# First attention block's outputs and last transposes moved into the MLP's PSUM banks, whole keys in 22 visits, a product at full height, 140 pairs of noughts, new ranks

## The chip, the cores and the metric

One Trainium2 chip, one core of it. The metric is device time in microseconds (us) of one execution. The kernel before takes 1190.74 us (median of three runs, 1190.32 to 1192.26). The profiled execution took 1190.45 us, its span from the first to the last instruction is 1188.7 us, so 1.75 us lie outside the span.

## The reference, cut to what matters

```
scores = (q @ k.T) / 8                                  # 4 batches, 8 heads, 576 rows, 64 wide
scores = where(scores >= rowmax(scores) - tau, scores, -1e9)
attn = exp(scores - rowmax(scores));  attn /= sum(attn) + 1e-9
x = (attn @ v), heads side by side                      # 2304 rows x 512
h = x @ w1_in;   g = max(h, 0) + alpha * min(h, 0);   x = g @ w1_out   # 512 -> 2048 -> 512
h = x @ w2_in;   g = h - tanh(h);                     out = g @ w2_out # 512 -> 2048 -> 512
```

Everything is computed in 32-bit floats.

## The kernel before

**Attention.** The 576 query rows of a head are cut into 256 + 256 + 64. A *visit* is one head and one block of 256 rows as two tiles of 128; 64 visits, numbered 0 to 63, eight heads to a block. Two heads' last 64 rows make one tile, a *left*; there are 16 of them. A tile goes through: scores on TensorE (`scores`, L644, lefts L730) into one of two PSUM tiles `sc` of two banks each; row maximum (L513), threshold (L516), exponential (L519, ScalarE), mask with row sum (L525), guard and reciprocal (L530, L533), scaling by the reciprocal; five transposes on TensorE, four into the bank `pt` (L569) and the last 64 keys' (L572) into the first bank of `sc`; copies out of PSUM; products with v (L663 or L671 and L672, lefts L753), written to `acc` for visits 0 to 7 and to the second bank of `sc` afterwards; then the output is put into `x`.

**Two ways to multiply.** A product in split form writes each operand as a high part (copy to the type fp32r) and a low part (the difference) and adds three fp32r products. A *raw* operand (`raw(k)`, `RAW` visits) is loaded whole and multiplied as float32 in one go; `one(k)` (`WHOLE` visits) does the same for v and the attention weights. With `raw` the copies `k_hi`, `k_lo` and the differences `q_lo`, `left_lo` fall away, with `one` `v_lo` and the low parts of the transposed weights. A float32 product shows as two TensorE records each.

**Weights of the MLPs.** Each MLP's weights come in 32 pieces of 512 KB, as raw 64-bit words (`piece`). A piece is made up by six steps; the two that only VectorE does are L347 (`ends_`) and L352 (`middle`), the differences are mostly GpSimd's (L284).

**MLP.** 18 blocks of 256 rows (9 in each MLP), eight *pairs* to a block. A pair is 24 first products into the bank `hp` (`h_pair`, L842), an activation on ScalarE and VectorE, a high and a low part, and the second products into the banks `acc` (`acc_pair`, L903 and L895). The first MLP's blocks run beside the attention of later blocks.

**Noughts.** `warm` multiplies zeros (`qc`) into `acc[1]`, two matmuls a time, 80 times (L960). They have the last rank of all and stand wherever the planner found nothing else for TensorE.

**The order.** Nothing is scheduled on the chip. `Plan.order` plays the program through with a cost for each operation, a lag between engines and a rank; at each step it issues the operation that can start first, the lowest rank among those, and so fixes the order of every engine's queue. Each queue, the loads' queue SP included, runs strictly in that order. The ranks are the numbers at the head of the file (`TA`, `PA`, `PB`, `MLP_PE`, `OFF` and so on). The planner also keeps two engines out of one PSUM bank at a time (the `banks` of an operation).

Of the kernel before, what the change touches and what calls it, by code (L numbers as in the profile page):

```python
# [37 lines left out]
TA = 17.2217  # L38
PA, PB = 8.596, 3.314
MLP_PE = 409.5389  # L40
MLP_G = -417.911
PREP = -31.4411
WHOLE = 17
RAW = 6
FLEX_R = 1
FLEX_HI = 1
POOL_PEN = 0.0393
ACT_PEN = 0
# [6 lines left out]
XR = 6.0872  # L55
FLEX = 1
T_WARM = 0.3
N_WARM = 80
DVE_PEN = 0.4374
OFF = {"S": 6.59, "M": -68.93, "TH": -138.48, "E": 14.87, "X": -28.47, "R": -62.2, "N": -8.46, "T": 123.89, "H": -217.07, "L": -80.02, "AV": 130.4, "XC": -36.36, "XH": -117.34}  # L60
# [169 lines left out]
def attention_mlp_mlp(ctx: ExitStack, tc: tile.TileContext, kv, q0, q1, tau, w1i, w1o, alpha, w2i, w2o, out):  # L230
# [30 lines left out]
    qc = tpool.tile([P, 2, P], F32R, name="qc")  # L261

# [26 lines left out]
    def either(dve, pool):  # L289
        return {"DVE": dve, "POOL": pool} if FLEX else {"POOL": pool}  # L290
# [101 lines left out]
    begun = {}  # L392

# [3 lines left out]
    def one(k):  # L397

        return whole(*visits[k])

    def raw(k):

        return k < RAW

    def prep(v, rank):
        b, qb, h = visits[v]
        k = brings[v]
        rkv, rq, ks, vs, qs = ("rkv", k), ("rq", v), ("ks", k), ("vs", k), ("qs", v)
# [26 lines left out]

        def k_hi(e):
            copy(e, take(tpool, ks, [P, 2, S], F32R, "ks", BUFS["ks"])[:, 0], T[rkv][:, :KW])
# [4 lines left out]
        def rows(x):  # L442
            return x[:, KW:].rearrange("p (c d) -> p c d", c=5)

        def v_hi(e):
            x = take(tpool, vs, [P, 5, 2, D], F32R, "vs", BUFS["vs"])[:, :, 0, :]
            copy(e, x.bitcast(F32) if one(k) else x, rows(T[rkv]))
# [25 lines left out]

        add({"SYNC": rate * QH}, rank - 6, load_q, [ROOM], [rq], takes=[("rq", rq)], lag=DMA_LAG)
        if new and raw(k):
            add({"SYNC": rate * KW}, rank - 6, load_whole_k, [ROOM], [(*ks, 0)], takes=[("ks", ks)], lag=DMA_LAG)
            add({"SYNC": rate * VW}, rank - 6, load_whole_v, [ROOM], [(*vs, 0)], takes=[("vs", vs)], lag=DMA_LAG)
        elif new:
            k_raw, v_raw = (*rkv, 0), (*rkv, 1)
            n = add({"SYNC": rate * KW}, rank - 6, load_k, [ROOM], [k_raw], takes=[("rkv", rkv)], lag=DMA_LAG)  # L480
            add({"SYNC": rate * VW}, rank - 6, load_v, [ROOM], [v_raw], lag=DMA_LAG, after=[n])
            add(any_of(0.58, 0.37, 0.64), rank, k_hi, [k_raw, ROOM], [(*ks, 0)], takes=[("ks", ks)])
            add(either(0.68, 1.42), rank, k_lo, [k_raw, (*ks, 0), ROOM], [(*ks, 1)])
# [3 lines left out]
        if qb:  # L487
            lc = ("qc", 0, h % 2)
# [3 lines left out]
        if new and not raw(k):  # L492
            add({"ACT": 0.36, "DVE": 0.4, "POOL": 0.5} if FLEX_HI else {"POOL": 0.5}, rank, v_hi, [v_raw, ROOM], [(*vs, 0)], takes=[("vs", vs)])
            if not one(k):
                add(either(0.4, 0.87), rank, v_lo, [v_raw, (*vs, 0), ROOM], [(*vs, 1)])

    HALVES = (slice(0, D), slice(D, P))
# [61 lines left out]

    def turned(tile, j, s, rank, g, g5, w, left, half):  # L560

        cols = slice(0, P) if left else slice(j * P, (j + 1) * P)
        p5 = sc[s][:D, :P]
        p5k, e0 = ("sc", s, "p5"), ("e", (tile, j))
        bank = [("sc", s, 0)]
# [12 lines left out]
        def pieces(x):  # L578
            return x.rearrange("p (c s) -> p c s", s=D)

        def hi_last(e):
            if g5 not in T:
                take(tpool, g5, [P, BLK], F32R, "eT5", BUFS["eT5"])
            x = T[g5][half] if left or w else T[g5][:D]
            if left and not w:
                copy(e, parts(x, 0), pieces(p5))
            else:
                copy(e, x[:, cols].bitcast(F32) if w else x[:, cols], p5)

        def lo_last(e):  # L590
            if left:
                sub(e, parts(T[g5][half], 1), pieces(p5), parts(T[g5][half], 0))
            else:
                sub(e, T[g5][D:P, cols], p5, T[g5][:D, cols])
# [23 lines left out]
        add({"PE": 0.06}, rank + OFF["T"], turn_last, [e0, ("const", 2), ROOM], [p5k], bank)  # L618
# [12 lines left out]
    def attend(v, rank):  # L631
# [15 lines left out]
        add({"PE": 1.05 if raw(k) else 0.8}, rank + OFF["S"], scores, [*ks_parts(k), *q_read, ROOM], [("sc", s, "s") for s in range(2)],  # L647
            [("sc", s, c) for s in range(2) for c in range(2)])
        softmax(v, 2, (0, 1), rank)
        pk, po = out_of(v)  # L650

        last = HALVES[pk[1]]
# [21 lines left out]
        add({"PE": 2.4 if w else 1.06}, rank + OFF["AV"], products, [*reads, ROOM], [pk, ("products", v)], pk_bank(pk))  # L674
# [22 lines left out]
        begun[xt] = add({"ACT": 0.38}, rank + OFF["XC"], x_copy, [pk, ROOM], [xk], pk_bank(pk),  # L697
                        takes=[("xt", xt)] if v % 2 == 0 else [], after=[begun[xt]] if v % 2 else [])
        if not w:
            add({"DVE": 0.4}, rank + OFF["XC"], x_add, [pk, ROOM], [xk], pk_bank(pk))  # L700
# [6 lines left out]
    def out_of(v):  # L707

        if v < H:
            return ("acc", v % 2), acc[v % 2][:, :BLK]  # L710
        return ("sc", v % 2, "po"), sc[v % 2][:, 768:]

    def pk_bank(pk):
        return [("acc", pk[1])] if pk[0] == "acc" else [("sc", pk[1], 1)]

    def attend_left(v, rank):
# [5 lines left out]

        def scores(e):
# [8 lines left out]
        reads = [x for k in ks_ for x in ks_parts(k)] + [("qc", 0, a) for a in range(2)] + [("const", 1)]  # L732
        add({"PE": sum(0.98 if raw(k) else 0.53 for k in ks_)}, rank + OFF["S"], scores, [*reads, ROOM], [("sc", s, "s")],
            [("sc", s, c) for c in range(2)])
# [96 lines left out]
    def h_pair(p, rank):  # L831
# [3 lines left out]
        for k in range(2):  # L835
            f = f0 + k
            for n0 in range(0, 12, 12 // GRP):
                now = todo[n0:n0 + 12 // GRP]

                def emit(e, now=now, n0=n0, k=k, f=f):  # L840
                    for n, (c, part, x) in enumerate(now):
                        e.matmul(  # L842
                            hp[:, k, :], lhsT=weight(l, "i", part, f // 4)[:, c, (f % 4) * P:(f % 4 + 1) * P],
                            rhs=T[f"x{x}", m][:, c, :], start=(n0 + n == 0), stop=(n0 + n == 11),
                        )

                reads = {("w", (l, "i", f // 4), c, part) for c, part, _ in now} | {(f"x{x}", m, c) for c, _, x in now}
                add({"PE": 0.118 * len(now)}, rank + MLP_PE, emit, sorted(reads, key=str), [("hp", 0)] + [("begun", m)] * (f == n0 == 0), [("hp", 0)])
# [35 lines left out]
    def acc_pair(p, rank):  # L884
        m, f0 = p // NPAIR, 2 * (p % NPAIR)
        l = m // NBLK
        for k in range(2):
            f = f0 + k
            for t in range(2):
# [20 lines left out]
                add({"PE": 0.705}, rank + MLP_PE, emit, [*reads, ("gh", p), ("gl", p)], [("acc", t)], [("acc", t)])  # L910
# [45 lines left out]
    add({"POOL": 0.46}, 0, clear, [], [("const", 1)] + [("qc", 0, a) for a in range(2)])  # L956
# [114 lines left out]
```

## Time and profile before

| | |
|---|---|
| median of three runs | 1190.74 us |
| profiled execution, its span | 1190.45 us, 1188.7 us |
| TensorE busy | 1152.9 us, 97% of the span |
| VectorE, ScalarE, GpSimd busy | 662.1, 650.9, 555.4 us |
| mean granted TensorE clock | 0.992 of 2.4 GHz |

The busy time of TensorE counts overlapping matmuls once, but it also counts matmuls that run at half the clock, and the noughts. What a stretch is worth must be read from the stretch: the attention of the first block comes first, with no MLP work to fill its waits; then attention and the first MLP run side by side until about 690 us; from there the MLPs are alone.

### The profile page before, as it was taken

To read this page: it belongs to the slowest core of one execution; us is meant where nothing else is said; L and a number is where in the kernel's file an instruction comes from. 1 tells how busy PE (TensorE), PEld (TensorE's weight loads), DVE (VectorE), ACT (ScalarE), POOL (GpSimd) and SP (SyncE) were. 2 spreads that over 40 slices of the span, in tenths; PEclk is the share of its full clock that TensorE was granted. 3 is DMA by queue.
4 is the path that set the end of the run, shared out by engine and by line. 5 is a ranking of instruction groups with operands and counts; after the bars stand their busy time and mean duration, and the time that the engine had idled before them with its cause. 6 is when DMAs were issued, how large, how long until landed. Compare 5 with 4: busy or idle time off the path is not lost.

```text
span 1188.7 us, 22011 instructions
## 1 busy us (share of the span) xinstructions
PE 1152.9 (97%) x8593; PEld 1045.4 (88%) x8593; DVE 662.1 (56%) x1393; ACT 650.9 (55%) x1265; POOL 555.4 (47%) x535
## 2 busy tenths in 40 slices
PE   9879998999999999999999999999999999999998
PEld 7548886999999989999999999999899899999997
DVE  6688785887878788778878666755111111111110
ACT  6677886666667767667666556665222222232221
POOL 4656664643645524556436366777232233223221
PEclk9889999999999999999999999999999999999999
DMA  7443432111113111122111144442010010010000
GB/s 219 133 151 103 135 113 77 56 58 41 59 39 90 57 48 38 54 63 73 55 41 55 36 148 151 156 154 89 2 36 22 15 36 12 25 37 1 19 18 18
DMA packets 51272, 81.13 MB, mean 68 GB/s; under 512 B 14560, under 2 KB 29920, under 8 KB 51168
## 3 DMA queue, kind: packets, MB, share of 16 engines
q1 hardware_dynamic: 51168, 79.73, 21.5%
q8 instruction: 67, 1.10, 0.4%
q14 instruction: 37, 0.30, 0.1%
HBM read 69.74 MB, written 9.96 MB: 67 GB/s over the span
## 4 chain that ended last, share of the span: by engine, by line
PE 86%; DVE 6%; ACT 4%; issue 2%; DMA 1%; POOL 0%; SPq 0%; ACTq 0%; DVEq 0%; POOLq 0%
PE hp L842 32%; PE acc L895 17%; PE acc L903 15%; PE sc L644 5%; PE pt L569 4%; PE sc L671 4%; PE sc L753 2%; ACT eT L279 2%; PE sc L663 1%; PE sc L572 1%; PE acc L663 1%; DVE e L525 1%; PE sc L730 1%; DVE st L513 1%; DVE rw L347 1%
## 5 line engine op out<-in xcount | busy, mean ns | idle before, releaser
L842 PE MATMUL hp<-x,ihi 128*128 128x256 f32 x2304 | 429.3, 285 | 1.6 <-DVE mr L863 1.6
L842 PEld LDWEIGHTS hp<-x,ihi 128*128 128x128 f32 x2304 | 358.2, 189 | 11.7 <-issue 2.8
L284 POOL TENSOR_TENSOR gl<-mr,gh 128x512 fp32r<-128x512 f32 x144 | 193.1, 1341 | 345.5 <-ACT gh L279 339.6
L842 PE MATMUL hp<-x,ilo 128*128 128x256 f32 x1152 | 323.7, 281 | 0.0
L861 DVE TENSOR_TENSOR mr<-hp,mr 128x512 f32<-128x512 f32 x72 | 49.8, 691 | 328.9 <-ACT mr L854 326.5
L842 PEld LDWEIGHTS hp<-x,ilo 128*128 128x128 f32 x1152 | 217.5, 189 | 0.0
L903 PE MATMUL acc<-gh,ohi 128*128 128x256 f32 x576 | 169.4, 294 | 0.0
L854 ACT ACTIVATE mr<-hp 128x512 f32<-128x512 f32 x72 | 43.1, 598 | 223.6 <-PE hp L842 223.6
L903 PE MATMUL acc<-gl,ohi 128*128 128x256 f32 x576 | 161.9, 281 | 0.0
L903 PE MATMUL acc<-gh,olo 128*128 128x256 f32 x576 | 161.6, 281 | 0.0
L513 DVE TENSOR_REDUCE st<-sc 128x1 f32<-128x576 f32 x144 | 106.4, 753 | 56.2 <-PE sc L644 33.4
L279 ACT ACTIVATE gh<-mr 128x512 fp32r<-128x512 f32 x133 | 84.0, 632 | 83.6 <-DVE mr L861 50.2
L525 DVE SCALAR_TENSOR_TENSOR e<-sc,st,e 128x576 f32<-128x576 f32 x144 | 115.9, 812 | 22.3 <-ACT e L519 13.6
L895 PE MATMUL acc<-ohi,gl 128*128 128x512 f32 x288 | 113.8, 395 | 0.0
L895 PE MATMUL acc<-olo,gh 128*128 128x512 f32 x288 | 113.7, 395 | 0.0
L895 PE MATMUL acc<-ohi,gh 128*128 128x512 f32 x288 | 113.5, 394 | 0.0
L519 ACT ACTIVATE e<-sc,st 128x576 f32<-128x576 f32 x144 | 104.9, 734 | 14.0 <-DVE st L513 11.3
L903 PEld LDWEIGHTS acc<-gh,ohi 128*128 128x128 f32 x576 | 108.7, 189 | 2.1 <-issue 2.0
L903 PEld LDWEIGHTS acc<-gl,ohi 128*128 128x128 f32 x576 | 108.7, 189 | 0.0
L903 PEld LDWEIGHTS acc<-gh,olo 128*128 128x128 f32 x576 | 108.5, 188 | 0.0
L279 ACT ACTIVATE eT<-pt 128x512 fp32r<-128x512 f32 (+1 forms) x144 | 85.6, 595 | 27.6 <-PE pt L569 23.0
L569 PE MATMUL pt<-ident,e 128*128 128x128 f32 x576 | 89.3, 278 | 8.1 <-ACT eT L279 3.9
(82 smaller groups left out, 1926.3 us busy)
## 6 DMA issues: line engine op xcount, KB each, us to landing
rkv<-in_kv_dram SPq DMA_DIRECT2D x50, 288.0 KB, 2.8
rw<-in_w1i_dram SPq DMA_DIRECT2D x16, 512.0 KB, 4.8
rw<-in_w1o_dram SPq DMA_DIRECT2D x16, 512.0 KB, 4.6
rw<-in_w2i_dram SPq DMA_DIRECT2D x16, 512.0 KB, 4.2
rw<-in_w2o_dram SPq DMA_DIRECT2D x16, 512.0 KB, 3.3
rkv<-in_kv_dram SPq DMA_DIRECT2D x50, 160.0 KB, 2.8
rq<-in_q_dram SPq DMA_DIRECT2D x160, 32.0 KB, 2.1
x1d<-o SPq DMA_DIRECT2D x18, 256.0 KB, 2.1
```

The lines of the kernel that those rows point to most:

```text
L279: e.activation(out=out_, in_=in_, func=AF.Copy, **({} if scale is None else {"scale": scale}))
L284: e.tensor_tensor(out=out_, in0=in_, in1=hi.bitcast(F32), op=ALU.subtract)
L513: e.tensor_reduce(out=T[st][:, 0, j:j + 1], in_=x(s), axis=AX.X, op=ALU.max, negate=True)
L519: e.activation(out=take(tpool, ("e", tile, j), [P, S], F32, "e", BUFS["e"]), in_=x(s), func=AF.Exp, bias=T[st][:, 0, j:j + 1], scale=1.0)
L525: e.scalar_tensor_tensor(out=w_, in0=x(s), scalar=T[st][:, 1, j:j + 1], in1=w_, op0=ALU.is_ge, op1=ALU.mult, accum_out=T[st][:, 2, j:j + 1])
L569: e.transpose(pt[:, c, :], T["e", tile, j][:, c * P:(c + 1) * P], ident)
L644: e.matmul(sc[j][:, 192:192 + S][:, c], lhsT=q_[p], rhs=k_[p, c], start=(n == 0), stop=(n == len(ops) - 1))
L671: e.matmul(po, lhsT=vf[:, c], rhs=T[g][part][:, c, :], start=(c + part == 0), stop=False)
L842: e.matmul(hp[:, k, :], lhsT=weight(l, "i", part, f // 4)[:, c, (f % 4) * P:(f % 4 + 1) * P], rhs=T[f"x{x}", m][:, c, :], start=(n0 + n == ...
L861: e.tensor_tensor(out=T[r], in0=hp, in1=T[r], op=ALU.subtract)
L895: e.matmul(acc[t], lhsT=g[:, k, t * P:(t + 1) * P], rhs=w, start=(f == 0 and n == 0), stop=(f == NF - 1 and n == 2),)
L903: e.matmul(acc[t][:, (c % 2) * BLK:(c % 2 + 1) * BLK], lhsT=w[:, c * P:(c + 1) * P], rhs=g[:, k, :], start=(f == 0 and n == 0 and c % 2 == ...
```

## The change

It sets `RAW` from 6 to 22 (keys and queries whole in visits 0 to 21) and `WHOLE` from 17 to 14. The lefts of the first batch take both heads' keys, loaded once more into a `rkv` buffer, 64 rows each, against a block-diagonal tile `qz` of 128 rows, in two float32 matmuls of 128 rows. In the first block both outputs lie in the bank `acc[0]`, side by side, and the last keys' transposes in `hp`, not in `sc`. In the lefts with split products, the last keys' weights lie high part over low part (128 rows) and are multiplied second, 64 columns wide, in place of 64 rows by 128 columns at the end. The noughts go from 80 pairs to 140, and all ranks and some of the planner's costs are other numbers. The diff, cut to its core:

```diff
-TA = 17.2217
-MLP_PE = 409.5389
-WHOLE = 17
-RAW = 6
+TA = 13.2318
+MLP_PE = 552.3152
+WHOLE = 14
+RAW = 22
...
-N_WARM = 80
+N_WARM = 140
...
+    qz = tpool.tile([P, P], F32, name="qz")
...
+        half = HALVES[h % 2] if raw(k) else slice(0, P)
+
         def left_hi(e):
-            x = qc[:, h % 2, col]
-            copy(e, x.bitcast(F32) if raw(k) else x, T[rq][:, P:], scale=qscale)
+            copy(e, qz[half, col] if raw(k) else qc[:, h % 2, col], T[rq][half, P:], scale=qscale[half])
...
+        def load_two(e):
+            x = take(tpool, kab, [P, KW + VW], F32, "rkv", BUFS["rkv"])
+            for a in range(2):
+                e.dma_start(out=x[HALVES[a], :KW], in_=kv[b, h + a][HALVES[a], :KW])
...
     def turned(tile, j, s, rank, g, g5, w, left, half):
 
         cols = slice(0, P) if left else slice(j * P, (j + 1) * P)
-        p5 = sc[s][:D, :P]
-        p5k, e0 = ("sc", s, "p5"), ("e", (tile, j))
-        bank = [("sc", s, 0)]
+        p5k, p5, bank = (("sc", s, "p5"), sc[s][:D, :P], [("sc", s, 0)]) if left or tile >= H else (("hp", s), hp[:D, s, :P], [("hp", 0)])
+        e0 = ("e", (tile, j))
...
         def lo_last(e):
-            if left:
-                sub(e, parts(T[g5][half], 1), pieces(p5), parts(T[g5][half], 0))
-            else:
-                sub(e, T[g5][D:P, cols], p5, T[g5][:D, cols])
+            sub(e, T[g5][D:P, cols], p5, T[g5][:D, cols])
...
     def out_of(v):
 
         if v < H:
-            return ("acc", v % 2), acc[v % 2][:, :BLK]
-        return ("sc", v % 2, "po"), sc[v % 2][:, 768:]
-
-    def pk_bank(pk):
-        return [("acc", pk[1])] if pk[0] == "acc" else [("sc", pk[1], 1)]
+            return ("acc", ("po", v % 2)), acc[0][:, v % 2 * BLK:][:, :BLK], HALVES[0], [("acc", 0)]
+        return ("sc", v % 2, "po"), sc[v % 2][:, 768:], HALVES[v % 2], [("sc", v % 2, 1)]
...
         def scores(e):
-            ops = []
-            for a, k in enumerate(ks_):
-                q_, k_ = qc[:, a], T["ks", k]
-                ops += [(q_[HALVES[s]].bitcast(F32), k_[HALVES[s], 0])] if raw(k) else [(q_, k_[:, 0]), (q_, k_[:, 1])]
+            if both:
+                ops = [(qz, T[kab])]
+            else:
+                ops = [(qc[:, a], T["ks", k][:, part]) for a, k in enumerate(ks_) for part in range(2)]
...
-                for c in range(5):
-                    e.matmul(
-                        dst, lhsT=vf[:, c] if c < 4 else vf[last, c],
-                        rhs=etf[:, c, c_] if c < 4 else et5f[last, c_], start=(c == 0), stop=(c == 4),
-                    )
+
+                for n, c in enumerate((0, 4, 1, 2, 3)):
+                    if c < 4:
+                        out_, l_, r_ = dst, vf[:, c], etf[:, c, c_]
+                    elif w:
+                        out_, l_, r_ = dst, vf[last, c], et5f[last, c_]
+                    else:
+                        out_, l_, r_ = dst[:, :D], vf[:, c], et5f[:, a * D:(a + 1) * D]
+                    e.matmul(out_, lhsT=l_, rhs=r_, start=(n == 0), stop=(n == 4))
```

The ranks move nearly every instruction. The first place is TensorE's queue in the first block. In the kernel before, from the last of the 160 noughts on, behind visit 4's scores, to visit 5's scores (L663 are products of visits 1, 2 and 3, L569 and L572 transposes, L644 scores):

```order
L960 MATMUL acc_92<-qc 128x256 x40
L663 MATMUL acc_92<-eT_303,vs 64x256 x4
L663 MATMUL acc_92<-eT_318,vs 64x256
L569 MATMUL pt<-ident,e 128x128 x4
L572 MATMUL sc_89<-ident,e 64x128
L572 MATMUL sc_90<-ident,e 64x128
L663 MATMUL acc_91<-eT_536,vs 64x256 x4
L663 MATMUL acc_91<-eT_542,vs 64x256
L569 MATMUL pt<-ident,e 128x128 x8
L663 MATMUL acc_92<-eT_584,vs 64x256 x4
L663 MATMUL acc_92<-eT_576,vs 64x256
L644 MATMUL sc_89<-ks,qs 128x320
```

And now, the same visit 4's scores (L655), visit 3's transposes (L589, L592) with noughts (L976) between them, and visit 3's products (L673):

```order
L655 MATMUL sc_90<-ks,qs 128x320
L655 MATMUL sc_91<-ks,qs 128x320
L655 MATMUL sc_90<-ks,qs 128x256
L655 MATMUL sc_91<-ks,qs 128x256
L589 MATMUL pt<-ident,e 128x128 x4
L592 MATMUL hp<-ident,e 64x128
L976 MATMUL acc_93<-qc 128x256 x2
L592 MATMUL hp<-ident,e 64x128
L976 MATMUL acc_93<-qc 128x256 x6
L589 MATMUL pt<-ident,e 128x128 x4
L976 MATMUL acc_93<-qc 128x256 x8
L673 MATMUL acc_92<-eT_531,vs 64x256 x4
```

Before, three visits' products stand between the scores of visits 4 and 5 and no nought comes after them; now each visit in the first block has this one pattern (scores, the visit before's transposes, its products), with 14 to 26 noughts among them, 230 up to the scores of visit 9, and the last of the 280 behind visit 12.

The second place is TensorE's queue at the products of the first left of the second batch. Before, with the transpose (L572) that follows:

```order
L753 MATMUL sc_90<-eT_3448,vs 128x128 x4
L753 MATMUL sc_90<-eT_3464,vs 128x128
L753 MATMUL sc_90<-eT_3448,vs 128x128 x4
L753 MATMUL sc_90<-eT_3464,vs 128x128
L572 MATMUL sc_90<-ident,e 64x128
```

And now:

```order
L771 MATMUL sc_91<-eT_3426,vs 128x128
L771 MATMUL sc_91<-eT_3437,vs 128x64
L771 MATMUL sc_91<-eT_3426,vs 128x128 x4
L771 MATMUL sc_91<-eT_3437,vs 128x64
L771 MATMUL sc_91<-eT_3426,vs 128x128 x3
L589 MATMUL pt<-ident,e 128x128 x4
```

Still ten matmuls; the two with 64 rows (the fifth and the tenth, which the order prints only by their output's shape) are now 128 rows high and 64 columns wide, and second of each five.

## Rows read from the trace of the kernel before

**Rows 1.** The page: busy time; granted clock and GB/s in 40 slices

```profile
PE 1152.9 (97%) x8593; PEld 1045.4 (88%) x8593; DVE 662.1 (56%) x1393; ACT 650.9 (55%) x1265; POOL 555.4 (47%) x535
...
PEclk9889999999999999999999999999999999999999
...
GB/s 219 133 151 103 135 113 77 56 58 41 59 39 90 57 48 38 54 63 73 55 41 55 36 148 151 156 154 89 2 36 22 15 36 12 25 37 1 19 18 18
```

**Rows 2.** Stretches: length, busy time by engine, granted clock, DMA share, GB/s

```profile
0.00:92.10 92.10, 77.19 (x433) 53.18 (x434) 64.50 (x124) 62.57 (x126) 50.32 (x56) 0.91 0.52 162
92.10:224.00 131.90, 126.57 (x986) 106.75 (x986) 100.11 (x207) 99.98 (x206) 79.68 (x80) 1.00 0.34 104
224.00:690.00 466.00, 456.42 (x3859) 432.24 (x3858) 363.74 (x898) 313.28 (x651) 225.66 (x259) 1.00 0.18 54
690.00:1188.70 498.70, 492.75 (x3321) 453.27 (x3319) 133.76 (x166) 175.07 (x286) 199.72 (x143) 1.00 0.17 55
```

**Rows 3.** Timeline of VectorE: start us, us; thresholds of tiles 0, 4, 5, 9, 24

```profile
8.86 0.23 DVE L516 TENSOR_SCALAR st<-st,atau 128x2 f32<-128x2 f32 x1
...
35.62 1.21 DVE L516 TENSOR_SCALAR st<-st,atau 128x2 f32<-128x2 f32 x1
...
58.74 0.61 DVE L516 TENSOR_SCALAR st<-st,atau 128x2 f32<-128x2 f32 x1
...
92.13 0.79 DVE L516 TENSOR_SCALAR st<-st,atau 128x2 f32<-128x2 f32 x1
...
224.14 0.38 DVE L516 TENSOR_SCALAR st<-st,atau 128x2 f32<-128x2 f32 x1
```

**Rows 4.** Chain that ended last, 0 to 100 us: start us, us, what

```profile
39.33 1.94 DMA rq<-in_q_dram
...
41.64 0.35 ACT qc L279
...
72.00 1.38 POOL ks L284
```

**Rows 5.** Timeline of TensorE in the first block: start us, us, instruction

```profile
17.89 1.24 PE L644 MATMUL sc<-ks,qs 64*128 64x320 f32 x8
...
33.13 5.04 PE L960 MATMUL acc<-qc 128*128 128x256 f32 x40
38.10 2.51 PE L663 MATMUL acc<-eT,vs 128*64 128x256 f32 x10
...
51.05 4.12 PE L663 MATMUL acc<-eT,vs 128*64 128x256 f32 x10 [0.97 <-ACT eT L279]
...
61.46 1.07 PE L644 MATMUL sc<-ks,qs 64*128 64x320 f32 x12
```

**Rows 6.** VectorE by line, 0 to 92.1 us: busy us, mean ns, idle before

```profile
L513 DVE TENSOR_REDUCE st<-sc 128x1 f32<-128x576 f32 x20 | 14.6, 750 | 11.5 <-PE sc L644 10.8 <-PE sc L572 0.7
L525 DVE SCALAR_TENSOR_TENSOR e<-sc,st,e 128x576 f32<-128x576 f32 x18 | 14.3, 814 | 6.7 <-ACT e L519 6.2
L347 DVE SCALAR_TENSOR_TENSOR rw<-rw 128x512 int32<-128x512 int32 x16 | 13.9, 867 | 2.8 <-ACT rw L342 1.5 <-POOL rw L344 1.3
L352 DVE SCALAR_TENSOR_TENSOR tw<-tw,rw 128x512 int32<-128x512 int32 x16 | 12.9, 809 | 0.7 <-DVE st L533 0.4
L516 DVE TENSOR_SCALAR st<-st,atau 128x2 f32<-128x2 f32 x9 | 3.8, 424 | 0.2
L530 DVE TENSOR_SCALAR st<-st 128x2 f32<-128x2 f32 x9 | 3.2, 359 | 0.2
```

**Rows 7.** Chain, 640 to 690 us

```profile
640.19 1.00 PE sc L644 x12
...
648.62 0.96 PE sc L671 x8
...
650.41 0.44 PE pt L569 x4
...
682.20 1.50 PE sc L753 x10
```

More of the change, by code (lines that the diff above doesn't have):

```diff
@@ L446, in v_hi @@
             x = take(tpool, vs, [P, 5, 2, D], F32R, "vs", BUFS["vs"])[:, :, 0, :]
-            copy(e, x.bitcast(F32) if one(k) else x, rows(T[rkv]))
+            copy(e, x, rows(T[rkv]))
         def v_lo(e):
@@ L487, in prep @@
         if qb:
-            lc = ("qc", 0, h % 2)
+            lc = ("qz" if raw(k) else "qc", 0, h % 2)
+            if raw(k) and h % 2 == 0:
+                add({"SYNC": rate * KW}, rank - 6, load_two, [ROOM], [(*kab, 0)], takes=[("rkv", kab)], lag=DMA_LAG)
             add({"ACT": 0.24}, rank, left_hi, [rq, ("const", 0), ROOM], [lc])
@@ L491, in prep @@
                 add({"DVE": 0.2}, rank, left_lo, [rq, ROOM], [lc])
[L492 to L497, printed above, removed]
+        if new and not one(k):
+            add(any_of(0.36, 0.4, 0.5), rank, v_hi, [v_raw, ROOM], [(*vs, 0)], takes=[("vs", vs)])
+            add(either(0.4, 0.87), rank, v_lo, [v_raw, (*vs, 0), ROOM], [(*vs, 1)])
     CHUNKS = (slice(0, 320), slice(320, S))
@@ L583, in hi_last @@
                 take(tpool, g5, [P, BLK], F32R, "eT5", BUFS["eT5"])
-            x = T[g5][half] if left or w else T[g5][:D]
-            if left and not w:
-                copy(e, parts(x, 0), pieces(p5))
-            else:
-                copy(e, x[:, cols].bitcast(F32) if w else x[:, cols], p5)
+            x = T[g5][half, cols].bitcast(F32) if w else T[g5][:D, cols]
+            copy(e, x, p5)
         def lo_last(e):
-            if left:
-                sub(e, parts(T[g5][half], 1), pieces(p5), parts(T[g5][half], 0))
-            else:
-                sub(e, T[g5][D:P, cols], p5, T[g5][:D, cols])
+            sub(e, T[g5][D:P, cols], p5, T[g5][:D, cols])
         def hi(e):
@@ L646, in attend @@
         q_read = [("qs", v, 0)] if raw(k) else [("qs", v, 0), ("qs", v, 1)]
-        add({"PE": 1.05 if raw(k) else 0.8}, rank + OFF["S"], scores, [*ks_parts(k), *q_read, ROOM], [("sc", s, "s") for s in range(2)],
+        add({"PE": 1.27 if raw(k) else 1.09}, rank + OFF["S"], scores, [*ks_parts(k), *q_read, ROOM], [("sc", s, "s") for s in range(2)],
             [("sc", s, c) for s in range(2) for c in range(2)])
         softmax(v, 2, (0, 1), rank)
-        pk, po = out_of(v)
-        last = HALVES[pk[1]]
+        pk, po, last, bank = out_of(v)
         reads = []
@@ L672, in products @@
             e.matmul(po, lhsT=vf[:, 4], rhs=T[g5], start=False, stop=True)
-        add({"PE": 2.4 if w else 1.06}, rank + OFF["AV"], products, [*reads, ROOM], [pk, ("products", v)], pk_bank(pk))
+        add({"PE": 2.4 if w else 1.06}, rank + OFF["AV"], products, [*reads, ROOM], [pk, ("products", v)], bank)
         m = 2 * b + qb
@@ L721, in attend_left @@
         g, g5 = ("eT", -v - 1), ("eT5", -v - 1)
+        both = all(raw(k) for k in ks_)
+        assert both or not any(raw(k) for k in ks_)
+        kab = ("rkv", -v - 1)
         def scores(e):
-            ops = []
-            for a, k in enumerate(ks_):
-                q_, k_ = qc[:, a], T["ks", k]
-                ops += [(q_[HALVES[s]].bitcast(F32), k_[HALVES[s], 0])] if raw(k) else [(q_, k_[:, 0]), (q_, k_[:, 1])]
+            if both:
+                ops = [(qz, T[kab])]
+            else:
+                ops = [(qc[:, a], T["ks", k][:, part]) for a, k in enumerate(ks_) for part in range(2)]
             for n, (q_, k_) in enumerate(ops):
@@ L730, in scores @@
                     e.matmul(sc[s][:, 192:192 + S][:, c], lhsT=q_, rhs=k_[:, c], start=(n == 0), stop=(n == len(ops) - 1))
-        reads = [x for k in ks_ for x in ks_parts(k)] + [("qc", 0, a) for a in range(2)] + [("const", 1)]
-        add({"PE": sum(0.98 if raw(k) else 0.53 for k in ks_)}, rank + OFF["S"], scores, [*reads, ROOM], [("sc", s, "s")],
-            [("sc", s, c) for c in range(2)])
+        reads = [(*kab, 0)] if both else [x for k in ks_ for x in ks_parts(k)]
+        reads += [("qz" if both else "qc", 0, a) for a in range(2)] + [("const", 1)]
+        add({"PE": 1.0 if both else 1.07}, rank + OFF["S"], scores, [*reads, ROOM], [("sc", s, "s")], [("sc", s, c) for c in range(2)])
         softmax(-v - 1, 1, (s,), rank)
```

61 lines of the change are left out of this document (35 added, 26 removed).

## The prediction

> **What bounds the kernel now.** I read the page first. TensorE is busy 97% of the span, the others half of it [rows 1], so time can only come from work TensorE needn't do, or from a place where its busy time is no use: noughts, and matmuls at half the clock. The clock row has such a place, the 8, 9 and 8 at the start [rows 1]. The table by stages then says how much: in the first 92.1 us TensorE is busy 77.2 us at a mean clock of 0.91; in the next 131.9 it idles 5.3 us, in the 466 after that 9.6 us, and in the last 498.7 us, the MLPs alone, 6 us, most of it the tail [rows 2]. So the later stages are TensorE's own work and the first one is not.
>
> What paces the first stage I read from VectorE's thresholds, one to a tile: tiles 0 to 4 go at (35.6 - 8.9) / 4 = 6.7 us each, the step to tile 5 takes 23.1 us, and tile 9 comes at 92.1, that is 8.4 us each for the last four [rows 3]. The reader is to see the cause of the gap in the chain: ScalarE's copy for the left queries (`qc`) stands in its queue ahead of visit 1's copies and waits for a load that lands at 41.3 us [rows 4], and behind it three visits' products go one after the other. With the noughts used up at 38.1 us (the last 40 end where the products begin) a float32 product takes 4.12 us where it took 2.51 [rows 5]; the stretch around it is where the clock row dips. No engine is full: VectorE is busy 64.5 of 92.1 us [rows 2] and waits mostly for scores and exponentials [rows 6].
>
> **The change part by part.**
>
> *The first block, up to tile 9's threshold.* The new order has one pattern per visit, no `qc` copy ahead of transposes, noughts until visit 12, no key copies or differences for visits 6 to 9 (one `ks` difference held GpSimd 1.38 us on the chain [rows 4]), and the last keys' transposes in another bank than the scores. VectorE's work to this point, counted in the new order: 20 maxima, 18 masks, 15 and 14 of the two weight steps, 10 thresholds, 9 guards. At the means per instruction (busy over count) of this stage [rows 6] that is 14.6 + 14.3 + 13.0 + 11.3 + 4.2 + 3.2 = 60.6 us, some 3 us more with reciprocals and the masks' accumulator reads, which have no row here; I take 63. It starts about 7 us in (the first threshold at 8.9 follows two maxima of 0.73 us), so tile 9 can't be before 70 us. From the other side, nothing may be won: 92. I take the pace that the trace shows where the noughts lasted, 6.7 us a visit with 1.25 pairs of weight steps each (5 in 4 visits by the order). Now there are 15 in 9 visits, 1.65. The 0.4 more, at 0.87 + 0.81 us, make 0.7 us, so 7.4 us a visit: 8.9 + 0.4 (the alphas' load now stands ahead of the first queries) + 9 x 7.4 = 76. Gain 16 us, between 0 and 22.
>
> Its cover: TensorE's own content up to there must stay under this. Eight float32 products at 2.51, ten raw scores at 1.24 [rows 5], eight visits' eight transposes at 0.11 [rows 7] are 20 + 12 + 7 = 39 us; 230 noughts at 4.97 / 40 = 0.124 us [rows 5] are 28.5. That is 68 us of the 76, so noughts are hidden in the waits only if these are where the planner thinks. If the pace were bounded elsewhere they cost nothing; if a wait is shorter than its noughts, up to 1 us a visit.
>
> *From tile 9 to tile 24 (132.0 us before [rows 3]).* The same attention work and the same MLP pairs by the order (516 first-size matmuls up to there in both). 50 noughts more, 6.2 us. They can fill the 5.3 us that TensorE idles there [rows 2]; between none and all, I take half, -2.6. Three visits' products leave float32: 2.51 becomes nine at 0.12 [rows 5, 7], -1.4 each, -4.3. Twelve more visits' scores, 10 to 21, become raw: in one view 1.24 against 1.07 [rows 5], +2.0. Their fall of VectorE and GpSimd work is off the path, as is the new low part of the three visits' weights: VectorE is busy 100 of 132 us [rows 2], some 7 us more fit. One left gets split products, -0.7 at most. Sum +0.6, between -5 and +5. The first batch's lefts take two 128-row float32 products; no row has that form, the nearest is 1.24 us for a raw visit's scores [rows 5]. I take no change, and 1 us either way for the four.
>
> *The lefts' products.* Twelve lefts. Ten matmuls take 1.50 us on the chain, while four transposes of the same 128 columns take 0.44, and nine products of 256 columns go at 0.12 each [rows 7]. At 0.11, ten would be 1.10. So the two with 64 rows cost 0.40 us a left beyond their length, and full height should return it: 12 x 0.40 = 4.8. Below: nothing, if the excess is a wait for the last copy. Above: with the two matmuls at half length, 0.11 more, 6.1 us.
>
> The Trainium skill (TensorEngine Tiling, Key Properties) says that a change of tiling mode drains TensorE. By that rule the 0.40 us is the drain at each of the two 64-row matmuls, and the whole of it goes; without it the excess could stay as a wait, and the term would be 0. The same skill (TensorE: Matmul & The Clock Gate, section LDWEIGHTS (loading the stationary operand)) gives loading the stationary operand a time that goes with its columns alone, 107 ns for 128, an estimate at its 1.2 columns per ns; the 0.11 us of the 128-column transposes [rows 7] agrees. By that rule the 64-column matmul is no shorter than the others, which speaks against the upper end, 6.1.
>
> *The rest.* From tile 24 the order is in step with the one before (within 24 first-size matmuls of MLP work at every third tile). Some 90 high parts of the MLP move from ScalarE to GpSimd; beside MLP work alone GpSimd is busy 200 of 499 us [rows 2], so two pairs ahead cover it. Nothing, between -3 and +3. If that cover is gone, the next late thing is a second product waiting on its low part.
>
> Sum against the profiled execution: 1190.45 - 16 + 0.6 - 4.8 = 1170. Its own time is 0.3 us under the median of the runs, which is nothing here.
>
> **The rivals.**
>
> *Loads set the pace (slower).* Up to tile 9 the new order must bring about 17 pieces of 512 KB, eight visits' keys, values and queries of 512 KB and the rest, some 13.8 MB; that takes 63 us at the 219 GB/s of the first slice, but 97 us at the 133 to 151 of the next two [rows 1]. Then tile 9 comes at 97, 5 us later than before, and the noughts behind it fill nothing: 1190.45 + 5 + 3.2 - 4.8 = 1194. It turns slower than before once tile 9 passes 94. For it: one queue issues every load and the raw keys go straight into it. Against it: the DMA share is 0.52 over that stage [rows 2], so those slices waited for buffers rather than for bandwidth.
>
> *The first block gains little.* The order's regularity is the planner's, and the chip's waits put the same 30-odd us back. Tile 9 at 88 to 92: 1182 to 1186. For it: at 6.7 us a visit VectorE was no fuller than later. Against it: the 23.1 us step is one misplaced wait and two slow products [rows 3 to 5], and both their causes are gone.
>
> *VectorE never waits.* Tile 9 at 70, and the better spaced order takes the idle 5.3 us too: 1190.45 - 22 - 3 - 6 = 1159.
>
> *No drain.* The lefts give nothing: 1175; inside the forecast's range.
>
> **How the numbers follow.** The forecast, 1164 to 1178 about 1170, 0.60; little gain, 1178 to 1188, 0.16; VectorE full, below 1164, 0.12; loads, slower, 0.12. About 2.4 us, 0.2%, is what a measurement here can tell from no change. Faster by more: 0.60 + 0.12 and nearly all of the 0.16, less a little, 0.84; within: 0.05; slower: 0.11. The range leaves out the slower case and the far end of the fast one: 1158 to 1189.
>
> **What would show it.** Right: tile 9's threshold at 71 to 82 us, tiles 0 to 9 in even steps of 7 to 8 us, no 8 in the clock row after the first slice, float32 products at 2.5 us throughout; tile 24 at 203 to 213; ten left products at 1.1 us on the chain; the last 500 us as they were. Wrong: thresholds that follow loads, TensorE waiting for SP's loads in the first 90 us; noughts on the chain beyond a few us, which would say they are longer than the waits; a left's products still at 1.5; a gain that is there at tile 24 and gone at tile 79.

## The result, and the profile after

The changed kernel takes 1180.68 us (median of 4 runs, 1180.2 to 1181.29) against 1191.13: ratio 0.9912, 95% interval 0.9895 to 0.9929, 10.4 us faster where 20.7 were forecast (1170 against the 1190.7 known then), and 2.7 us above the range of 1164 to 1178. The profiled execution took 1180.95 us, its span 1179.2.

The page of the changed kernel, the rows that answer to [rows 1]:

```profile
PE 1150.1 (98%) x8620; PEld 1049.2 (89%) x8620; DVE 678.1 (58%) x1388; ACT 575.0 (49%) x1132; POOL 602.9 (51%) x640
...
PEclk9999999999999999999999999999999999999999
...
GB/s 192 181 151 165 150 103 73 58 24 60 39 59 90 58 25 55 43 91 55 42 41 55 41 186 134 127 162 90 1 36 37 1 37 27 11 36 7 13 19 18
```

The dip in the clock row is gone. ScalarE does 76 us less work, GpSimd 48 us more, VectorE 16 us more.

Timeline of VectorE, thresholds of tiles 0, 4, 5, 9 and 24 of the changed kernel, against [rows 3]:

```profile
10.18 0.23 DVE L536 TENSOR_SCALAR st<-st,atau 128x2 f32<-128x2 f32 x1
...
41.55 0.23 DVE L536 TENSOR_SCALAR st<-st,atau 128x2 f32<-128x2 f32 x1
47.84 0.63 DVE L536 TENSOR_SCALAR st<-st,atau 128x2 f32<-128x2 f32 x1
...
78.47 0.70 DVE L536 TENSOR_SCALAR st<-st,atau 128x2 f32<-128x2 f32 x1
...
212.21 0.23 DVE L536 TENSOR_SCALAR st<-st,atau 128x2 f32<-128x2 f32 x1
```

The 23.1 us step is gone, tile 9 comes at 78.5 instead of 92.1. The chain of waits in the first block, against [rows 4]:

```profile
5.23 6.41 DMA rw<-in_w1i_dram
...
15.93 1.81 DVE tw L353
...
20.78 2.44 PE acc L673 x10
23.22 1.17 PE sc L655 x8
24.39 0.67 PE acc L976 x4
```

No copy for left queries is on it and no GpSimd difference of keys; a float32 product takes 2.44 us each time on this chain, which is the 2.51 of the timeline in [rows 5]. What is new here is a wait for the first weight piece, 6.41 us, ahead of visit 1. Further on the chain has a left's products, 1.50 us in [rows 7], as

```profile
653.62 1.26 PE sc L771 x10
```

A threshold stands in VectorE's queue, and at tile 24 it comes 2.6 us after the tile's first score matmul before, 6.7 us after it now. So I account for the time at TensorE's own marks: the first score matmul of tiles 9 and 24, the last product of the last left, the end. The MLP matmuls issued up to tile 24's mark are 516 in both. Stretches between these marks, first of the kernel before (us, busy time of TensorE, its weight loads, VectorE, ScalarE, GpSimd, granted clock, DMA share, GB/s):

```profile
0.00:88.60 88.60, 74.42 (x410) 51.10 (x410) 61.33 (x117) 59.61 (x119) 47.91 (x53) 0.90 0.54 168
88.60:221.50 132.90, 126.85 (x984) 106.52 (x983) 101.05 (x211) 101.32 (x208) 80.00 (x80) 1.00 0.33 101
221.50:683.40 461.90, 452.32 (x3829) 428.03 (x3828) 364.49 (x898) 311.34 (x645) 225.05 (x256) 1.00 0.18 54
683.40:1188.70 505.30, 499.35 (x3374) 459.80 (x3373) 135.25 (x170) 178.63 (x293) 202.42 (x147) 1.00 0.17 55
```

and of the changed kernel:

```profile
0.00:75.20 75.20, 72.08 (x470) 55.57 (x470) 57.26 (x111) 52.51 (x107) 39.02 (x51) 1.00 0.63 188
75.20:205.50 130.30, 127.36 (x961) 108.34 (x960) 105.12 (x211) 94.35 (x194) 78.04 (x83) 1.00 0.40 121
205.50:672.70 467.20, 450.05 (x3814) 424.82 (x3814) 378.93 (x899) 294.11 (x609) 241.11 (x289) 1.00 0.18 52
672.70:1179.20 506.50, 500.59 (x3381) 460.49 (x3380) 136.84 (x170) 134.04 (x222) 244.74 (x218) 1.00 0.17 55
```

| stretch | before, us | after, us | difference | forecast |
|---|---|---|---|---|
| to tile 9's scores | 88.6 | 75.2 | -13.4 | -16 |
| to tile 24's scores | 132.9 | 130.3 | -2.6 | +0.6 |
| to the last left's products | 461.9 | 467.2 | +5.3 | -4.8 |
| to the end | 505.3 | 506.5 | +1.2 | 0 |

Up to tile 24 the gain is 16.0 us, against a forecast of 15.4. The shortfall is all behind it: the third stretch was to get 4.8 us shorter and got 5.3 longer, with TensorE idle for 467.2 - 450.05 = 17.2 us instead of 9.6. In VectorE's column about as many instructions (898 and 899) take 14 us more.

### The profile page after: what moved, and what is told of

It is laid out like the page before. It is cut to its first block, busy times and chain, and to the rows that moved or that the text cites. A ratio compares the mean times of both kernels' runs of the same rounds, so it can differ in the third digit from the quotient of the medians.

```text
span 1179.2 us, 22125 instructions
## 1 busy us (share of the span) xinstructions
PE 1150.1 (98%) x8620; PEld 1049.2 (89%) x8620; DVE 678.1 (58%) x1388; ACT 575.0 (49%) x1132; POOL 602.9 (51%) x640
## 4 chain that ended last, share of the span: by engine, by line
PE 78%; DVE 11%; ACT 4%; issue 3%; POOL 2%; DMA 1%; SPq 0%; ACTq 0%; DVEq 0%; POOLq 0%
PE hp L857 30%; PE acc L910 17%; PE acc L918 13%; PE sc L655 4%; PE pt L589 4%; PE sc L681 3%; DVE e L545 3%; DVE eT L285 2%; DVE st L533 1%; PE sc L592 1%; PE sc L771 1%; DVE st L550 1%; PE acc L673 1%; PE acc L976 1%; DMA rw<-in_w1i_dram 1%
## 5 line engine op out<-in xcount | busy, mean ns | idle before, releaser
L282 POOL TENSOR_SCALAR gh<-mr 128x512 fp32r<-128x512 f32 x100 | 63.3, 633 | 299.4 <-DVE mr L876 215.9
L533 DVE TENSOR_REDUCE st<-sc 128x1 f32<-128x576 f32 x144 | 106.3, 753 | 38.6 <-PE sc L655 23.1
L280 ACT ACTIVATE e<-e,st 128x576 f32<-128x576 f32 x97 | 72.9, 770 | 61.1 <-DVE st L553 60.1
L280 ACT ACTIVATE eT<-pt 128x512 fp32r<-128x512 f32 (+1 forms) x144 | 85.4, 593 | 30.6 <-PE pt L589 26.4
```

The costliest lines, as they stand in the source:

```text
L280: e.activation(out=out_, in_=in_, func=AF.Copy, **({} if scale is None else {"scale": scale}))
L282: e.tensor_scalar(out=out_, in0=in_, scalar1=1.0, scalar2=1.0, op0=ALU.mult, op1=ALU.mult)
L533: e.tensor_reduce(out=T[st][:, 0, j:j + 1], in_=x(s), axis=AX.X, op=ALU.max, negate=True)
```

## The experiments

In each, "before" is the kernel before on the same chip (1190.1 to 1191.1 us); ratios are to it, with their 95% intervals. "The stage" is the third stretch of the table, taken at the same marks, in one trace of each kernel. The tile marks given below are VectorE's thresholds, other than where TensorE's are named. Since the kernel before ranges over 1 us from set to set, smaller differences between runs of different sets aren't told apart.

### The lefts' products in either order

In the kernel before, only the lefts' last keys as in the changed kernel:

```diff
-    for c in range(5): e.matmul(dst, lhsT=vf[:, c] if c < 4 else vf[last, c], ...)
+    for n, c in enumerate((0, 4, 1, 2, 3)): ...  # c == 4: dst[:, :D], lhsT=vf[:, 4], rhs=et5f[:, a * D:(a + 1) * D]
```

> The kernel before, its order untouched, with only the lefts' last keys changed: copied at full height and multiplied with 128 rows. If TensorE's time in the stage of tiles 24 to 79 is the time of that stage (theory A, the prediction's), 12 lefts give back 0.40 us each: about 1186.3 against 1191.1, ten left products at 1.1 us on the chain, and idle time of TensorE as before (8.9 us between tiles 24 and 79). If the saved time turns into waits whatever the order (theory B), 1191 within 1 us, with the products at 1.1 us and 4 to 5 us more idle. If the saving isn't there at all (theory C), the products stay at 1.5 us.

1187.7 us, ratio 0.998 (0.9971 to 0.999). The stage takes 458.1 us instead of 461.9.

The reverse, the changed kernel with the old lefts' products:

> The changed kernel, its order untouched, with the old lefts' products (last keys at half height). Theory A: 4.5 to 4.8 us slower than the changed kernel, 1185.3. Theory B, that this order's waits take the saving: 0 to 1 us slower, 1181 to 1182, with 4 to 5 us less idle of TensorE between tiles 24 and 79 than the 15.1 us of the changed kernel.

1183.0 us, 0.9935 (0.9923 to 0.9947), 2.4 us over the changed kernel. The stage takes 469.1 us instead of 467.2. So the saving is real in both orders (theory C falls), in the stage's traces 3.8 us in the old and 1.9 in the new: TensorE's busy time falls by 5.6 and 3.4 us, and 1.8 and 1.5 of that becomes idle time. By the medians it is 2.4 us in either, so whether the orders differ in it is open. The excess stood at the matmuls of 64 rows: in the stage's lefts TensorE's next matmul starts 0.12 us after a 128-row one, but the 64-row one starts 0.205 us after the one ahead of it, and the one behind it 0.254 us after it. And with either kind of lefts the new order is slower in this stage: 469.1 against 461.9, 467.2 against 458.1, that is 7.2 to 9.1 us for nearly the same matmuls (visits 20 and 21 take eight records for their scores in place of twelve, and six second products of the MLP lie behind the last mark instead of ahead of it).

### Noughts

```diff
     def warm(e):
+        warmed.append(0)
+        if len(warmed) > 80: return
```

> The changed kernel with the 60 last pairs of noughts issuing nothing, all else in its order. If the noughts after the first 80 pairs stand on the path (theory D), those up to tile 9 go (some 70 matmuls of 0.12 us, of which the chain shows about half): tile 9 comes 3 to 6 us earlier than 78.5 and the time is 1175 to 1178. If they hold the clock (theory E, the prediction's), the clock row shows an 8 or less in the third slice, float32 products of the visits after the 80th pair take up to 4.1 us instead of 2.4, and tile 9 comes 2 to 8 us later, 1183 to 1189. Hidden in waits and not needed for the clock: 1181 within 1 us.

1179.4 us, 0.9904 (0.9891 to 0.9917); tile 9 at 77.4, tile 24's scores 2.9 us earlier than in the changed kernel, clock row all 9. In this run the last 60 pairs cost 1 to 3 us (the ratios' intervals overlap) and the clock didn't need them. Another run without them, in the section on late transposes, has an 8 in the second slice, so that is not shown to hold every time. Without any:

> The changed kernel without any noughts. If only the first 80 pairs hold the clock (theory E in its weaker form, after the run without the last 60): an 8 or less in the first three slices of the clock row, float32 products of the first visits at 4 to 5 us instead of 2.4, tile 9 at 84 to 95, the time 1186 to 1196. If the clock needs none of them: tile 9 at 70 to 76 and the time 1172 to 1178.

1183.7 us, 0.9945 (0.9926 to 0.9964); tile 9 at 81.2, tile 24 at 212.8. The page:

```profile
PE   4778999999999999999999999999999999999998
...
PEclk9899999999999999999999999999999999999999
```

One slice at 8; two of the first block's eight products take 4.07 and 4.64 us in the timeline, the others 2.51. That is a loss of 2.7 us at tile 9 that is down to 0.6 at tile 24. The six runs lie between 1180.4 and 1188.9, where the changed kernel's four lie within 1.1 us: the noughts buy an even clock more than time.

### The first weight pieces

The two first pieces' loads behind visit 1's, and their steps behind a mark in tile 0 or tile 1:

```diff
+    for group, mark in ((early_loads, behind["v", 1]), (early_steps, behind["mask", 0, 1])):  # second run: behind["thr", 1]
+        ...  # those that stood ahead of the mark follow it
```

> The changed kernel with the loads of the first two weight pieces behind visit 1's query, key and value, and piece 0's first step behind tile 0's two masks; nothing else moves. If that wait costs the first visits 4.7 us (tile 1's threshold at 19.1 against 14.4 before) and the shift is carried on (theory F): tile 1 at 15 to 16, tile 9 at 74.5 to 76, the time 1177 to 1178. If a later limit takes it back (theory G: VectorE's own work and the noughts set the pace from there): tile 1 at 15 to 16, tile 9 at 78 to 79, the time 1180 to 1181.

1183.3 us, 0.9937 (0.9924 to 0.995). A miss: tile 1 stays at 19.2. ScalarE's two steps still stood ahead of visit 1's query copy, which came at 14.9 us. The marks of this trace, the fastest of five runs, lie within 0.7 us of the changed kernel's; why the median is 2.6 us over it is open. With all steps behind tile 1's threshold:

> As the run with the first pieces' loads moved, but all steps of the first two pieces stand behind tile 1's threshold: ScalarE's two steps no longer stand ahead of visit 1's query copy, nor VectorE's ahead of visit 0's guard. In that earlier run the query copy still came at 14.9 us, behind ScalarE's steps that wait for the loads, and tile 1 at 19.2. Theory F2: tile 1's threshold at 16 to 17.5 (the 48 noughts between the first two visits' scores, 6 us, are the next bound), tile 9 at 76 to 77, the time 1178 to 1179.5. Theory G: tile 1 earlier, tile 9 unchanged at 78 to 79, the time 1180 to 1182.

1185.7 us, 0.9955 (0.994 to 0.997). Tile 1 comes at 17.3, but tile 2 at 31.9 instead of 26.4. TensorE's timeline in this run shows why:

```profile
22.97 4.72 PE L673 MATMUL acc<-eT,vs 128*64 128x256 f32 x10 [3.46 <-ACT eT L280]
27.61 2.29 PE L655 MATMUL sc<-ks,qs 64*128 64x320 f32 x8
```

The moved steps now hold ScalarE's copy of visit 0's second transposes; TensorE waits for it: it stands idle for 3.46 us, and the product and scores behind that wait take 4.72 and 2.29 us where the same forms take 2.51 and 1.24 in the changed kernel's timeline: the granted clock there is 0.50, that is 1.2 instead of 2.4 GHz (the clock row begins with 8). In this trace, the slowest of five runs, the shift is carried to the end, tile 9 at 85.1.

> The same, with 24 noughts instead of 48 between the first two visits' scores (as before) and none after the 80th pair. If loads, noughts and the pace add up (theories D and F2): tile 1 at 14.5 to 16, tile 9 at 73.5 to 75.5, tile 24 at 205 to 207, the time 1174.5 to 1177. If VectorE's work sets the pace whatever goes on ahead: tile 9 at 77 to 78, the time 1178.5 to 1180. If the clock needs the noughts: an 8 in the clock row's first three slices, and no gain.

1184.4 us, 0.9946 (0.9931 to 0.9961): tile 1 at 14.2, tile 2 at 29.2, tile 9 at 85.4, 8 in the first and third slice. The early wait is real but can't be had by moving these steps alone.

### Parts, ranks and the last keys' bank

The changed kernel with the old ranks, offsets and penalties, and the kernel before with the new ones:

> The changed kernel planned with the ranks, offsets and penalties of the kernel before (its raw keys, whole weights, 140 pairs of noughts, last keys' banks and lefts' products kept). Theory H, from the first two runs (the old order with new lefts needs 446.3 us between tiles 24 and 79, the new order 450.7): the ranks give back the time there. Then that stage takes 446 to 447; if the first block's gain is the parts' and not the ranks', tile 9 stays at 76 to 82 and the time is about 1176. Theory I, that the first block's even pace comes from the ranks: tile 9 at 86 to 92 and the time 1184 to 1190. Theory J, that the parts and not the ranks cost the later stage: it stays at 450 to 451.

> The kernel before planned with the new ranks, offsets and penalties alone. Theory H: tile 24 to 79 takes 452 to 453, 2 to 3 us more than the 449.8 of before (the old lefts hide part of the new order's waits). Theory I: tile 9 comes at 80 or earlier, the time 1180 to 1184. If the parts make the first block: tile 9 at 88 to 92, the time 1190 to 1194.

1209.0 us (1.0156, 1.0137 to 1.0174) and 1202.8 (1.0098, 1.0085 to 1.0111). Tile 9 comes at 84.3 and 89.1, and from tile 24's threshold to tile 79's it takes 463.1 and 460.8 us, against 449.8 and 450.7 in the two kernels. By TensorE's marks tile 9's scores stand at 77.2 and 85.4 (before 88.6, changed 75.2): of the first block's 13.4 us the new parts bring 11.4 in the old order's ranks, the new ranks alone 3.2. The run with the new parts has lost that again at tile 24's scores (227.7, before 221.5). Both are slower than either kernel, so theory H in its plain form (the ranks carry the loss) falls: ranks and parts belong together, and undoing one of them makes a third order instead of telling the two apart.

```diff
-    ... hp[:D, s, :P], [("hp", 0)])
+    ... sc[s][:D, :P], [("hp", 0)])
```

> The changed kernel with the last keys' transposes of the first eight visits back in the scores' banks, the order untouched. If the other bank is what lets the visits overlap: tile 9 2 to 6 us later than 78.5, the time 1183 to 1187. If the order alone decides (the columns don't overlap with the scores'): tile 9 at 78 to 79, the time within 1 us of the changed kernel's.

1183.6 us, 0.9945 (0.9933 to 0.9958), tile 9 at 81.8. The other bank is worth 3.3 us of the first block.

### TensorE's late transposes

TensorE's named waits in the stage of the changed kernel (total us, times, longest):

```profile
PE sc L592 <- ACT xt L280: 5.5, 10, 0.7
PE pt L589 <- ACT e L280: 4.2, 5, 1.4
PE sc L681 <- DVE st L533: 2.3, 3, 0.8
PE pt L589 <- POOL e L560: 1.2, 3, 0.6
```

The wait for the normalised weights `e` was 0.7 us, once, before:

```profile
PE pt L569 <- ACT e L279: 0.7, 1, 0.7
```

In TensorE's queue alone, 17 such transposes were put behind the MLP work that follows them:

> The changed kernel, and on TensorE alone 13 last-key transposes that waited 0.3 to 0.7 us each for ScalarE are put behind the next piece of MLP work (0.7 us), and 4 first transposes that waited 0.6 to 1.4 us behind the next two pieces; the other engines' order stays. Theory K, that these waits are only TensorE standing in front of a late input with MLP work ready behind it: TensorE's idle time between tiles 24 and 79 falls from 15.1 us to 5 to 8, that stage takes 442 to 445 us instead of 450.7, the time is 1172 to 1176. Theory L, that the softmax chain paces the stage and the wait comes back at the next step: idle within 2 us of 15, time 1179 to 1182.

1183.9 us, 0.9946 (0.9934 to 0.9958): 3 us slower. From tile 24's threshold to tile 79's the idle time falls from 17.1 to 16.0 us (the 15.1 of the expectation is only what the named waits add up to) and the time grows from 450.7 to 454.2. Theory K falls: who steps aside is late at the next step. The same without the last 60 pairs of noughts takes 1184.6, with 1182.6 to 1188.6 in six runs; its trace has an 8 in the clock row's second slice and a product of 3.86 us. So the softmax chain itself had to be looked at.

### What holds the softmax chain

The longest of these waits in the trace of the changed kernel. VectorE's pieces on the chain of waits there, start and us:

```profile
390.21 1.27 DVE st L550
391.48 1.36 DVE qs L464
392.84 0.09 DVE st L553
```

GpSimd's timeline beside it:

```profile
390.01 1.45 POOL L285 TENSOR_TENSOR ks<-rkv,ks 128x576 fp32r<-128x576 f32 x1
391.41 1.28 POOL L285 TENSOR_TENSOR gl<-mr,gh 128x512 fp32r<-128x512 f32 x1
```

and TensorE's:

```profile
393.78 0.66 PE L589 MATMUL pt<-ident,e 128*128 128x128 f32 x4 [1.40 <-ACT e L280]
```

The guard (L550, an addition of 1e-9 to 128x2 sums) lasts until GpSimd's first operation ends at 391.46, the low part of the queries (L464) until 0.15 us after its second ends at 392.69. Then come the reciprocal, ScalarE's normalising, and TensorE, which has waited 1.40 us. VectorE by line and shape in the stage, before:

```profile
L516 DVE TENSOR_SCALAR st<-st,atau 128x2 f32<-128x2 f32 x44 | 19.0, 431 | 0.9
...
L530 DVE TENSOR_SCALAR st<-st 128x2 f32<-128x2 f32 x45 | 13.5, 301 | 0.8
```

and in the changed kernel (the last row is the guard of the lefts, on one column):

```profile
L550 DVE TENSOR_SCALAR st<-st 128x2 f32<-128x2 f32 x45 | 21.6, 480 | 1.1
L536 DVE TENSOR_SCALAR st<-st,atau 128x2 f32<-128x2 f32 x44 | 20.2, 458 | 0.6
...
L553 DVE RECIPROCAL st<-st 128x2 f32<-128x2 f32 x45 | 7.3, 163 | 1.1
...
L550 DVE TENSOR_SCALAR st<-st 128x1 f32<-128x1 f32 x12 | 1.8, 152 | 0.3
```

In the whole trace a two-column guard that starts beside a GpSimd operation takes 0.64 us (41 of them, up to 1.36), one that doesn't 0.165 (23); thresholds 0.75 and 0.23. All 35 two-column guards over 0.3 us end 0.02 to 0.03 us after a GpSimd operation. On one column the guard takes 0.15 and the threshold 0.21 either way, and the two-column reciprocal 0.16. In the stage 26 of 57 guards take over 0.3 us, 13 before. Of VectorE's 14 us more in the stage the guards are 8, the thresholds 1 and the low parts of the queries (L464) nearly 5. So write both small operations by columns:

```diff
-            e.tensor_scalar(out=T[st][:, 3], in0=T[st][:, 2], scalar1=1e-9, ...)
+            for j in range(n):
+                e.tensor_scalar(out=T[st][:, 3, j:j + 1], in0=T[st][:, 2, j:j + 1], scalar1=1e-9, ...)
```

and the threshold likewise.

> The changed kernel with VectorE's threshold and guard written as two operations on one column each instead of one on two columns; nothing moves. In the changed kernel's trace the guard on 128x2 takes 0.165 us while GpSimd idles and 0.64 us on average, up to 1.36, while GpSimd runs (41 of 64 guards), and the threshold 0.23 and 0.79; the same operations on 128x1 take 0.15 and 0.21 whatever GpSimd does. Theory M, that GpSimd's added work holds these two small operations, and through them the softmax chain and TensorE: no guard over 0.2 us, TensorE's idle time from tile 24's scores to the last product (205.5 to 672.7 us, 17.2 us idle) falls by 4 to 8 us, the time is 1174 to 1177. Theory N, that the order's other waits take their place: the guards are short, the idle time falls by less than 2 us, the time is 1180 to 1182.

1166.1 us (1165.3 to 1166.6), 0.9789 (0.977 to 0.9807): 14.6 us faster than the changed kernel, more than theory M asked for. Stage, VectorE and TensorE's waits in this run:

```profile
204.30:658.20 453.90, 446.65 (x3814) 424.19 (x3814) 359.99 (x988) 294.53 (x609) 241.51 (x289) 1.00 0.18 54
```

```profile
L537 DVE TENSOR_SCALAR st<-st,atau 128x1 f32<-128x1 f32 x100 | 17.0, 207 | 0.6
L552 DVE TENSOR_SCALAR st<-st 128x1 f32<-128x1 f32 x102 | 13.0, 148 | 0.3
```

```profile
PE sc L594 <- ACT xt L280: 3.9, 10, 0.5
PE pt L591 <- ACT e L280: 0.5, 2, 0.3
```

The stage falls from 467.2 to 453.9 us, TensorE's idle time from 17.2 to 7.3, the wait for `e` from 4.2 to 0.5, though GpSimd does the same 289 operations. The same edit in the kernel before:

> The same edit in the kernel before, where 21 of 57 guards between tile 24's scores and the last product fall beside GpSimd's work instead of 33. Theory M: 1 to 3 us faster, 1187.5 to 1189.5 against 1190.5. Theory N: within 1 us of it.

1187.0 us, 0.9965 (0.9949 to 0.9981); the stage 460.9 instead of 461.9, tile 9's scores 3.8 us earlier. (Part of that may be the clock: in this trace the products of visits 2 and 3 take 3.21 and 2.51 us, 4.15 and 4.12 before, and its runs lie between 1181.6 and 1193.2.) The held guards and thresholds cost the old order 1 us in the stage, the new one 13.3.

> The changed kernel with the guard alone by columns (both together: 1166.1 against 1180.7). The guard stands between the masks and the reciprocal, the normalised weights and TensorE's transposes. If it is the one that TensorE waits for: 9 to 13 of the 14.6 us, 1168 to 1172. If the threshold, ahead of the masks, is it: 1177 to 1181.

> The changed kernel with the threshold alone by columns. The other side of the same question: 1177 to 1180 if the guard is what TensorE waits for, 1168 to 1172 if the threshold is. If neither alone brings its part (the wait then only passes from one to the other), both runs stay above 1176.

1169.5 us (0.9824, 0.981 to 0.9839) and 1176.3 (0.9884, 0.9868 to 0.9901): 11.1 and 4.4 us under the changed kernel, 15.5 together where both at once gave 14.6. The guard is the larger, and the two add. With the high parts off GpSimd instead:

> The changed kernel with every high part of the MLP's activations on ScalarE (GpSimd made 100 of 144), in the place where it stood. It takes 20 GpSimd operations of 0.62 us out of the stage of tiles 24 to 79. Theory M: fewer guards beside GpSimd's work, 1 to 3 us faster, 1177.5 to 1179.5. Theory N, or ScalarE's queue late in turn: 1180 to 1184, with new waits for ScalarE.

1179.2 us, 0.9896 (0.9877 to 0.9914). Guards over 0.3 us fall from 26 to 19, but the stage stays at 467.7, and the ratio's interval overlaps with the changed kernel's: it isn't the high parts' number that matters. Which GpSimd operations the guards meet is the order's, and it isn't settled why the new order meets twice as many and has so much less room for it.

> The column-wise threshold and guard together with the noughts left out after the 80th pair (that run: 1179.4). Theory M: 1172 to 1176; theory N: 1179 to 1181.

1164.0 us (1162.9 to 1165.7), 0.9773 (0.9754 to 0.9793), the fastest of all, though its interval overlaps with that of the columns alone.

## Why the prediction was half right

- **First block, -16.** Right in its mechanism. From tile 1 to tile 9 the pace is (78.5 - 19.1) / 8 = 7.4 us a visit, as forecast; tile 0 comes 0.9 us later than counted and the step to tile 1 takes 8.9 us, since weight steps waiting for their loads stand ahead of visit 1's query copy, and since one of VectorE's, ahead of tile 1's maxima, takes 1.81 us on the chain where 0.69 is the least, beside a GpSimd operation from 15.90 to 17.17. Tile 0 and this step together are the missing 2.4 us. I had counted the weight steps' length, and neither their loads nor such a hold. One reading of the kernel before was off: the copies behind `qc` [rows 4] are visit 2's. Visit 1's were done by 22.0 us, and its products at 38.1 only stood behind the noughts.
- **Noughts.** "Hidden in the waits" holds to 1 to 3 us. Their use for the clock is shown, but small: without any, two of the first eight products were slow and the median rose by 3 us.
- **Tile 9 to 24, +0.6.** It was -2.6; the two terms together gain 16.0 us against 15.4. The terms of this sum were not tested one by one. The threshold as a mark hid 4 us of the gain.
- **Lefts, -4.8.** The mechanism is right (10 products at 1.07 to 1.28 us on the chain, and TensorE's busy time falls by 3.4 to 5.6 us), the size is not: 1.9 us of the stage in the new order, 3.8 in the old, 2.4 by the medians of either. The sum took TensorE's saved time for the stage's, although TensorE had waits there already. The step behind a 64-column matmul is 0.08 us against 0.12, so it is shorter; the prediction had taken it for no shorter when it spoke against its upper end.
- **The rest, 0 within 3.** This step failed: it cost 7.2 to 9.1 us in the stage and 1.2 in the tail. I read "in step" from counts of matmuls on TensorE's queue, and asked of GpSimd only whether it had time for the added work. What counted is what its operations stand beside: VectorE's guard and threshold, held until GpSimd is done, on the way from the scores to TensorE's transposes. With both by columns the stage of the new order is 7.0 us shorter than the old one's (453.9 against 460.9), not 5.3 longer. Of the tail's 1.2 us some 0.7 are the six second products that now lie in it, at 0.12 us each; the rest is open. The rows showed it: thresholds of 1.21, 0.61 and 0.79 us beside 0.23 [rows 3], means of 424 and 359 ns for 256 numbers [rows 6]. I used the means as the price of the operation and didn't ask why single ones differ fivefold.
- **The rivals.** Loads set the pace: no, tile 9 at 78.5 with a DMA share of 0.63. Little gain in the first block: the time fell into the bracket given to it (1178 to 1188), but its mechanism didn't come. VectorE never waits, no drain: no. What the prediction named as a sign against it, a gain there at tile 24 and gone at tile 79, is what came, by a third.

With guard and threshold by columns in both kernels the difference is 1187.0 - 1166.1 = 20.9 us, near the 20.7 forecast. That is luck in part and no proof of each term: in the traces it is -14.4 us up to tile 24's scores, -7.0 in the stage and +1.2 behind it, where -15.4, -4.8 and 0 were forecast.

## What to carry to other kernels

Before counting what an engine has room for, look at the spread of its smallest operations: one that takes 0.165 us alone and 1.36 in company is waiting for another engine, and may do so on the path. Writing it in another shape is a cheap test. A change that moves work between GpSimd and another engine is priced by what VectorE does meanwhile. Compare stages at marks in the bounding engine's own queue: marks on VectorE hid 4 of 16 us here.

## What the runs showed of the hardware

- The guard, a VectorE addition from SBUF to SBUF on two columns, waits until GpSimd's running operation ends (0.165 us alone, up to 1.36 beside it); on one column it doesn't (0.15), nor does a reciprocal on two (0.16), nor the 128x576 maximum from PSUM (0.75 either way). Held in the same way were the threshold on two columns (up to 1.16 us), the low parts of the queries (0.34 alone, up to 1.46) and the weights' steps on 128x512 (0.68 alone, up to 2.42). The Trainium skill (SBUF — State Buffer, section SBUF: two separate sides) has the rule behind it: VectorE and GpSimd have one pair of ports in common, which one of them holds for its whole instruction, VectorE only with operations of some forms. The guard's end at 391.48 and GpSimd's at 391.46 agree with it.
- Two float32 products of a left with the 64-row matmul second of five take 1.87 us on the chain (20 records), with it last 1.73.
- In the lefts with split products a 64-row matmul among 128-row ones starts 0.205 us after the one ahead of it, and the one behind it 0.254 us later; between 128-row ones it is 0.12.
